# Covariance made the other way round and scaled by a row from DRAM, in place of a turn on TensorE

## The chip, the cores and the metric

The kernel runs on one core of a Trainium2 chip. Its time is the device time of one execution in microseconds (us); lower is better. The engines are PE (TensorE), DVE (VectorE), ACT (ScalarE), POOL (GpSimd) and SP (SyncE, which here only issues DMAs). Each takes its own instructions in program order; semaphores order them between engines.

## The reference

Two layers, one after the other, for 4 batches of 6208 rows with 256 channels, in float32:

```python
qn = q / (norm(q, axis=1) + 1e-06)             # norms down the 6208 rows, one for each channel
kn = k / (norm(k, axis=1) + 1e-06)
s  = kn.transpose(0, 2, 1) @ qn / tau           # [4, 256, 256], tau = 1
a  = softmax(s, axis=-1)
x  = v @ a                                      # [4, 6208, 256]

x_prev = x shifted down by one row
xk = mu_k * x + (1 - mu_k) * x_prev
xr = mu_r * x + (1 - mu_r) * x_prev
out = sigmoid(xr @ w_r) * (relu(xk @ w_k) ** 2 @ w_v)      # w_k 256 x 1024, w_v 1024 x 256, w_r 256 x 256
```

The softmax of a batch needs all rows of its q and k, and no row of x of that batch can be made before it.

## The kernel before

Batch 0 is handled by itself at the start. After that the kernel goes through 48 blocks of 512 rows (12 in a batch) and one short block of the rows left over. The order of all work is written out by hand: for each block `i` there are 8 slots `j`, and in each slot the main loop calls a fixed list of small pieces. A slot takes about 1.2 us, a block about 9.6 us.

For a block, `x_half` multiplies the turned v by the softmax (`xT_ps`, L458, with `a_sb` as the weights), ACT moves the result to SBUF (L460), DVE makes `delta` (L539), `xk` and `xr` (L549), `up` makes one eighth of the first product (`kT_ps`, L564), ACT applies relu (`kr`, L569), DVE squares (`kk`, L577), `down` makes the second product and the gate (`vr_ps`, L592 and L596), and `finish` combines them (ACT L605, DVE L606). Stores (L613) and the DMA transpositions of v (L410) go through SP's queue; loads of v (L402) and of q and k (L133) through POOL's. `x_half` of block n is called in slots 0 and 2 of step n-2, so it runs ahead of the rest of its block. `xT_ps`, `bank` and `st_ps` share two buffers of PSUM; `vr_ps` has two, `kT_ps` three.

The covariances of batches 1 to 3 are spread between the blocks of the batch ahead: `unit_matmul` adds 128 rows at a time into `s_ps` (L293), with q as the weights, so that S has q's channels down the partitions and k's along the columns. `unit_square` (ACT) and the adds on DVE gather the sums of squares.

When the last unit of a batch is through, `softmax_pieces` gives a list of small pieces (`chain`), and each following slot runs one of them, ahead of the slot's other work:

```python
        return [evac, None, norms, roots, pow2, None, invert, None, None, turn, lambda: exp([0]), lambda: exp([1]),
                shares, lambda: weigh(0), lambda: weigh(1)]
```

`evac` copies S from PSUM to `s_sb` (ACT, L346). `norms` sums the squares over the partitions on PE (L309), `roots` copies them to `rn` (ACT, L313), `pow2` takes the root on POOL (L335). `invert` adds 1e-6, takes the reciprocal (DVE, L338 and L339), and scales the rows of `s_sb` by q's inverse norms (L341, twice). `turn` transposes `s_sb` in four matmuls against the identity into `st_ps` (L353), so that k's channels lie down the partitions. `exp` reads `st_ps` with k's inverse norms as the scale of each partition (ACT, L361), and its sums go to `sm`. `shares` inverts the sums (DVE, L366), and `weigh` writes one half of `a_sb` (ACT, L370). `None` is a slot in which the chain does nothing. The chain also pauses when it has `NORMS` pieces left until the sums of squares are complete.

Of the kernel before, what the change touches and what calls it, by code (L numbers as in the profile page):

```python
# [10 lines left out]
F32 = mybir.dt.float32  # L11
BF16 = mybir.dt.bfloat16
AX = mybir.AxisListType.X
AF = mybir.ActivationFunctionType
OP = mybir.AluOpType
# [3 lines left out]
def kernel(  # L19
# [13 lines left out]
    nc = tc.nc  # L33
    B, N, C = q.shape
    D = C
    DF = moe_w_k.shape[1]
    P = 128
# [12 lines left out]
    pn = ctx.enter_context(tc.tile_pool(name="pn", bufs=2))  # L50
    p2 = ctx.enter_context(tc.tile_pool(name="p2", bufs=3))
    ps = ctx.enter_context(tc.tile_pool(name="ps", bufs=1, space=bass.MemoryType.PSUM))
    ctx.enter_context(tc.manual_schedule())

    ident = const.tile([P, P], BF16, name="ident")
# [23 lines left out]
    st_ps = {}  # L79
# [10 lines left out]
    def sizes(b):  # L90
        return [1] + [S] * (NB - 1) + [S // 2] * 2 if b == 0 else [1] + [S] * NB

    def order(b):
        g = list(range(len(sizes(b))))
        return [1, 2, 0] + g[3:]

    def rows_of(b, g):
        return (P if g else L), sizes(b)[g]
# [8 lines left out]
    def apart(b, g):  # L107
        return b == 1 and g > 0

    def rows_at(qk, b, g, i):  # L110
        if apart(b, g):
            return qk.rearrange("p s i c -> p (s i c)").rearrange("p (i s c) -> p i s c", i=2, s=S)[:, i]
        return qk[:, :, i]
# [169 lines left out]
    def unit_matmul(b, g, s):  # L283
        rows, n = rows_of(b, g)
        t0 = g == order(b)[0] and s == 0
        te = g == len(sizes(b)) - 1 and s == n - 1
        if t0:

            cov[b] = ps.tile([P, 2, C], F32, name="s_ps", tag="s_ps")
        s_ps = cov[b]  # L290
        qk = groups[b, g][0]
        for ih in range(2):
            nc.tensor.matmul(s_ps[:, ih, :], rows_at(qk, b, g, 0)[:rows, s, ih * P:(ih + 1) * P],  # L293
                             rows_at(qk, b, g, 1)[:rows, s, :], start=t0 and ih == 0, stop=te,
                             skip_group_check=True)
    def softmax_pieces(b):

        s_ps = cov.pop(b) if b else None
        rn = pn.tile([P, 4], F32, name="rn")
        s_sb = pn.tile([P, 2, C], F32, name="s_sb")  # L300
        e_sb = pn.tile([P, 2, C], F32, name="e_sb", bufs=1)
        mx = pn.tile([P, 2], F32, name="mx")
        sm = pn.tile([P, 2], F32, name="sm")
        rk = rn[:, 2:4]
        def norms():
            bank[b] = ps.tile([P, 4], F32, name="bank", tag="xT_ps", bufs=2)
            t = sums.pop(b)
            for i in range(4):
                nc.tensor.matmul(bank[b][:, i:i + 1], t[:, i * P:(i + 1) * P], ones[:, 0:1],  # L309
                                 start=i == 0, stop=True, skip_group_check=True)  # L310

        def roots():
            nc.scalar.copy(rn, bank[b])  # L313

        def diagonals():
            dg = pn.tile([P, 2, P], F32, name="dg", tag="dg", bufs=1)
            for h in range(2):
                nc.vector.scalar_tensor_tensor(dg[:, h], cov[0][h][:, 3 * P * h:3 * P * h + P], 1.0, ident_f,
                                               op0=OP.mult, op1=OP.mult, accum_out=rn[:, h:h + 1])

        def root(h):
            nc.scalar.activation(rn[:, 2 * h:2 * h + 2], bank[0][:, 0:2] if h else rn[:, 0:2], AF.Sqrt)

        def invert_first(h):
            nc.vector.tensor_scalar_add(rn[:, 2 * h:2 * h + 2], rn[:, 2 * h:2 * h + 2], 1e-6)
            nc.vector.reciprocal(rn[:, 2 * h:2 * h + 2], rn[:, 2 * h:2 * h + 2])
            if h and inv_tau != 1.0:
                nc.vector.tensor_scalar_mul(rk, rk, inv_tau)

        def evac_first():  # L330
            for h in range(2):
                nc.vector.tensor_scalar_mul(s_sb[:, h], cov[0][h][:, P:P + C], rn[:, h:h + 1])

        def pow2():
            nc.gpsimd.tensor_tensor(rn, rn, half, op=OP.pow)  # L335

        def invert():
            nc.vector.tensor_scalar_add(rn, rn, 1e-6)  # L338
            nc.vector.reciprocal(rn, rn)  # L339
            for h in range(2):  # L340
                nc.vector.tensor_scalar_mul(s_sb[:, h], s_sb[:, h], rn[:, h:h + 1])  # L341
            if inv_tau != 1.0:
                nc.vector.tensor_scalar_mul(rk, rk, inv_tau)

        def evac():
            nc.scalar.copy(s_sb, s_ps)  # L346

        def turn():

            st_ps[b] = ps.tile([P, 2, C], F32, name="st_ps", tag="xT_ps", bufs=2)  # L350
            for n in range(4):
                ih, dh = divmod(n, 2) if b else (n % 2, n // 2)
                nc.tensor.transpose(st_ps[b][:, ih, dh * P:(dh + 1) * P], s_sb[:, dh, ih * P:(ih + 1) * P],  # L353
                                    ident_f)

        def exp(halves=range(2)):
            for ih in halves:
                if not bounded:
                    nc.vector.tensor_reduce(mx[:, ih:ih + 1], st_ps[b][:, ih], axis=AX, op=OP.max, negate=True)
                    nc.vector.tensor_tensor(mx[:, ih:ih + 1], mx[:, ih:ih + 1], rk[:, ih:ih + 1], op=OP.mult)  # L360
                nc.scalar.activation(e_sb[:, ih], st_ps[b][:, ih], AF.Exp, scale=rk[:, ih:ih + 1],  # L361
                                     bias=0.0 if bounded else mx[:, ih:ih + 1],
                                     accum_out=sm[:, ih:ih + 1])

        def shares():
            nc.vector.reciprocal(sm, sm)  # L366

        def weigh(ih):
            ready.add((b, ih))
            nc.scalar.activation(a_sb[:, b, ih, :], e_sb[:, ih], AF.Copy, scale=sm[:, ih:ih + 1])  # L370

        def weigh_first(ih):
            nc.vector.reciprocal(sm[:, ih:ih + 1], sm[:, ih:ih + 1])
            nc.vector.tensor_scalar_mul(a_sb[:, b, ih, :], e_sb[:, ih], sm[:, ih:ih + 1])

        if b == 0:
            return diagonals, root, invert_first, evac_first, turn, exp, weigh_first

        return [evac, None, norms, roots, pow2, None, invert, None, None, turn, lambda: exp([0]), lambda: exp([1]),
                shares, lambda: weigh(0), lambda: weigh(1)]  # L380

    blocks = [(b, t) for b in range(B) for t in range(NB)] + ["left"]
    NBLK = len(blocks)
# [269 lines left out]
    def keep_warm(n):  # L653

        junk_ps = ps.tile([P, M], F32, name="junk_ps", tag="kT_ps", bufs=3)
        for _ in range(n):
            nc.tensor.matmul(junk_ps, ones, fill, start=True, stop=True)

    diagonals, root, invert_first, evac_first, turn, exp, weigh_first = softmax_pieces(0)
    pending = []  # L660
    for g in (1, 3, 5):
# [36 lines left out]
            pos["ld"] += 1  # L698

    chain = []  # L700
    NORMS = 13
    holds = [0]
    added = [0]

    def unit(ahead=2):

        if pos["mm"] >= len(units):
            return
        u = units[pos["mm"]]
        loads_upto()  # L710
        feed(max(ahead, 1))
        unit_matmul(*u)
        pos["mm"] += 1
        feed(ahead)
        if u[1:] == (NB, S - 1):
            chain.extend(softmax_pieces(u[0]))
            holds[0] = u[0]
# [46 lines left out]
    for i in range(-2, NBLK - 1):  # L764
        for j in range(8):
# [7 lines left out]
            if chain:  # L773
                piece = chain[0]
                if len(chain) == NORMS and (any(e[1] == holds[0] for e in adds) or now[0] < added[0] + 3):
                    piece = None
# [23 lines left out]
            if 0 < i + 2 < NBLK:  # L800
                n = i + 2
# [19 lines left out]
            if i == -1 and j in (5, 6):  # L821
                for u in early[:2] if j == 5 else early[2:]:
                    unit_matmul(*u)
# [60 lines left out]
```

## Time and profile before

| what | value |
|---|---|
| runs | 504.22 us median of 3 (503.79 to 505.19) |
| the profiled execution | 503.88 us, its span 502.1 us |
| TensorE clock granted | full over the whole span |
| PE / DVE / ACT / POOL busy | 96% / 85% / 85% / 19% of the span |
| DMA, mean over the span | 166 GB/s in 131542 packets |

The span is what the hardware profiler saw of one execution; about 1.8 us lie around it. A busy share is an average over the whole span: between about 45 and 495 us PE is busy almost without a gap, at the start it waits for the inputs. In the timelines two starts in a row on an engine can lie closer together than the first one's length, since instructions overlap in part; what an instruction takes away from its engine is the time to the next start.

### The profile page before, as it was taken

The page shows a single profiled execution, that of the slowest core. Times are in us where ns is not written, and L with a number is a line of the kernel's source. Part 1 is how long each engine was busy: PE and PEld are TensorE (multiplying, and loading weights), DVE is VectorE, ACT ScalarE, POOL GpSimd, SP SyncE. Part 2 cuts the span into 40 slices and gives each one's busy share as a digit, 9 for nine tenths or more (in the row PEclk, how much of TensorE's full clock was granted, in tenths as well). Part 3 has the DMA queues.
Part 4 walks back from the last instruction along what each step waited for, and adds up shares of the span by engine and source line. Part 5 has one row for each costly group of instructions (what it writes and reads, how often), then busy time and mean ns, then how long its engine had stood idle before and what let it go on. Part 6 is the DMA issues. An engine that isn't in the chain of part 4 may idle for free.

```text
span 502.1 us, 9301 instructions
## 1 busy us (share of the span) xinstructions
PE 481.3 (96%) x3437; PEld 331.0 (66%) x3437; DVE 428.4 (85%) x786; ACT 428.7 (85%) x872; POOL 96.6 (19%) x142
## 2 busy tenths in 40 slices
PE   1789999999999999999999999999999999999996
PEld 0355677667666766766776676676666666666675
DVE  2778899999988998998989899899898787878794
ACT  3789998999899889889998898998888888788884
POOL 0043421222333132121223323100031010000000
PEclk9999999999999999999999999999999999999999
DMA  8999999999799999997599999972296657345123
GB/s 325 418 315 197 201 193 174 211 208 199 146 184 184 200 168 180 148 196 121 139 188 154 190 175 180 177 140 64 75 198 104 152 90 153 77 107 85 58 69 106
DMA packets 131542, 83.46 MB, mean 166 GB/s; under 512 B 50532, under 2 KB 125608, under 8 KB 130472
## 3 DMA queue, kind: packets, MB, share of 16 engines
q0 software_dynamic: 55824, 33.01, 49.7%
q1 hardware_dynamic: 75352, 49.59, 40.0%
q8 instruction: 27, 0.44, 0.4%
q10 hardware_dynamic: 320, 0.26, 0.2%
q14 instruction: 19, 0.16, 0.1%
HBM read 78.71 MB, written 25.43 MB: 207 GB/s over the span
## 4 chain that ended last, share of the span: by engine, by line
PE 91%; DMA 4%; ACT 2%; DVE 1%; issue 1%; SPq 1%; ACTq 0%; DVEq 0%
PE vr_ps L596 33%; PE kT_ps L564 33%; PE vr_ps L592 8%; PE xT_ps L458 8%; PE s_ps L293 6%; DMA f<-in_k_dram 3%; ACT k L160 1%; DMA v_bf<-in_v_dram 1%; SPq L125 1%; ACT qk L155 0%; PE y_ps L636 0%; PE st_ps L353 0%; DVE k L167 0%; PE kT_ps L504 0%; DVE k L170 0%
## 5 line engine op out<-in xcount | busy, mean ns | idle before, releaser
L569 ACT ACTIVATE kr<-kT_ps 128x512 bf16<-128x512 f32 (+1 forms) x390 | 234.5, 604 | 33.2 <-PE kT_ps L564 29.5
L596 PE MATMUL vr_ps<-w_v_sb,kk 128*128 128x256 bf16 x1536 | 230.3, 273 | 0.0
L564 PE MATMUL kT_ps<-xk,w_k_sb 128*128 128x512 bf16 (+1 forms) x780 | 229.8, 377 | 0.0
L596 PEld LDWEIGHTS <-kk 128*128 128x128 bf16 x1536 | 150.3, 98 | 57.3
L577 DVE TENSOR_TENSOR kk<-kr 128x2048 bf16<-128x2048 bf16 (+1 forms) x148 | 125.6, 850 | 0.2 <-ACT kr L569 0.2
L606 DVE SCALAR_TENSOR_TENSOR res<-res,vr_ps 128x256 f32<-128x256 f32 x192 | 79.8, 416 | 50.1 <-ACT res L605 50.1
L564 PEld LDWEIGHTS <-w_k_sb 128*128 128x128 bf16 x780 | 75.5, 98 | 27.5 <-issue 0.6
L605 ACT ACTIVATE res<-vr_ps 128x256 f32<-128x256 f32 x192 | 76.5, 398 | 1.3 <-PE vr_ps L596 1.3
L592 PE MATMUL vr_ps<-w_r_sb,xr 128*128 128x256 bf16 x384 | 73.3, 273 | 0.0
L460 ACT CAST xT<-xT_ps 128x512 bf16<-128x512 f32 x94 | 55.9, 595 | 20.0 <-PE xT_ps L458 19.6
L549 DVE SCALAR_TENSOR_TENSOR xk<-delta,mu_t,xT 128x512 bf16<-128x512 bf16 x94 | 69.9, 745 | 0.0
L549 DVE SCALAR_TENSOR_TENSOR xr<-delta,mu_t,xT 128x512 bf16<-128x512 bf16 x94 | 69.9, 745 | 0.0
L592 PEld LDWEIGHTS <-xr 128*128 128x128 bf16 x384 | 37.6, 98 | 44.6 <-issue 0.2
L133 POOL DMA_DIRECT2D qk<-in_q_dram x39 | 26.1, 669 | 168.2 <-ACT kr L569 138.2
L458 PE MATMUL xT_ps<-vT,a_sb 128*128 128x512 bf16 x188 | 55.9, 379 | 0.0
L293 PE MATMUL s_ps<-qk 128*128 128x256 bf16 (+1 forms) x294 | 55.8, 273 | 0.0
L402 POOL DMA_DIRECT2D v_bf<-in_v_dram x48 | 36.6, 764 | 97.0 <-DMA vT<-v_bf 47.9
L254 ACT ACTIVATE sq<-qk 128x1024 bf16<-128x1024 bf16 x48 | 51.0, 1063 | 0.0
L199 PE MATMUL s_ps<-qk 128*128 128x384 bf16 (+2 forms) x98 | 20.0, 355 | 15.1 <-ACT qk L155 15.1
L539 DVE TENSOR_TENSOR delta<-xT 128x1024 bf16<-128x1024 bf16 x47 | 32.2, 685 | 0.7 <-ACT xT L460 0.7
L293 PEld LDWEIGHTS <-qk 128*128 128x128 bf16 (+1 forms) x294 | 28.5, 98 | 5.6 <-issue 0.8
L133 POOL DMA_DIRECT2D qk<-in_k_dram x39 | 25.9, 665 | 3.8 <-DMA w_k_sb<-in_moe_w_k_dram 2.4
(113 smaller groups left out, 249.5 us busy)
## 6 DMA issues: line engine op xcount, KB each, us to landing
out_dram<-res SPq DMA_DIRECT2D x47, 512.0 KB, 4.8
v_bf<-in_v_dram POOLq DMA_DIRECT2D x48, 256.0 KB, 7.1
qk<-in_q_dram POOLq DMA_DIRECT2D x36, 256.0 KB, 6.2
qk<-in_k_dram POOLq DMA_DIRECT2D x36, 256.0 KB, 7.8
f<-in_q_dram SPq DMA_DIRECT2D x4, 1024.0 KB, 13.4
f<-in_k_dram SPq DMA_DIRECT2D x4, 1024.0 KB, 11.0
f<-in_q_dram SPq DMA_DIRECT2D x3, 512.0 KB, 7.7
f<-in_k_dram SPq DMA_DIRECT2D x3, 512.0 KB, 6.1
```

The lines of the kernel that those rows point to most:

```text
L133: nc.gpsimd.dma_start(rows_at(qk, b, g, i)[:rows, :n], qk_src(t, b, g))
L293: nc.tensor.matmul(s_ps[:, ih, :], rows_at(qk, b, g, 0)[:rows, s, ih * P:(ih + 1) * P], rows_at(qk, b, g, 1)[:rows, s, :], start=t0 and ih ...
L458: nc.tensor.matmul(xT_ps, a_sb[:, b, ih, dh * P:(dh + 1) * P], vT[:, :, ih, :], start=ih == 0, stop=ih == 1)
L460: nc.scalar.copy(xT[:, dh, 1:], xT_ps)
L549: nc.vector.scalar_tensor_tensor(o[:, dh], st[i, "d"][:, dh], mu[:, dh:dh + 1], st[i, "x"][:, dh, :M], op0=OP.mult, op1=OP.add)
L564: nc.tensor.matmul(kT_ps[:, :m], w_k_sb[:, dh, fh * P:(fh + 1) * P], xk[:, dh, :m], start=dh == 0, stop=dh == 1)
L569: nc.scalar.activation(kr, kT_ps[:, :m], AF.Relu, scale=0.5 ** 0.5)
L577: nc.vector.tensor_tensor(st[i, "kk"][:, fh // 4 * 4 + lo:fh + 1, :m], kr, kr, op=OP.mult)
L592: nc.tensor.matmul(vr_ps[:, D:], xr[:, dh, s * P:(s + 1) * P], w_r_sb[:, dh, :], start=dh == 0, stop=dh == 1)
L596: nc.tensor.matmul(vr_ps[:, :D], kk[:, fh, s * P:(s + 1) * P], w_v_sb[:, fh, :], start=fh == 0, stop=fh == 7)
L605: nc.scalar.activation(res[:, s], vr_ps[:, D:], AF.Tanh, scale=0.5)
L606: nc.vector.scalar_tensor_tensor(res[:, s], res[:, s], 1.0, vr_ps[:, :D], op0=OP.add, op1=OP.mult)
```

## The change

For batches 1 to 3 the operands of the covariance matmuls are exchanged, so that S comes out with k's channels down the partitions and q's along the columns. It needs no turn, and `exp` reads it from `s_sb`. q's inverse norms now belong to the columns: `invert` writes them from `rn` to a row of 256 numbers in DRAM, and reads that row back to all 128 partitions (`rq`), with two DMAs on SP's queue. Five slots after `invert`, a new piece `spread` multiplies `s_sb` by `rq` on DVE, in one instruction. The two scalings in `invert` go. The two `exp` follow `spread`, `shares` and the first `weigh` are joined in one piece, and the chain has 16 pieces instead of 15. Batch 0 is unchanged.

```diff
+    scratch = ctx.enter_context(tc.tile_pool(name="scratch", bufs=2, space=bass.MemoryType.DRAM))
...
         for ih in range(2):
-            nc.tensor.matmul(s_ps[:, ih, :], rows_at(qk, b, g, 0)[:rows, s, ih * P:(ih + 1) * P],
-                             rows_at(qk, b, g, 1)[:rows, s, :], start=t0 and ih == 0, stop=te,
+            nc.tensor.matmul(s_ps[:, ih, :], rows_at(qk, b, g, 1)[:rows, s, ih * P:(ih + 1) * P],
+                             rows_at(qk, b, g, 0)[:rows, s, :], start=t0 and ih == 0, stop=te,
                              skip_group_check=True)
...
+        rq = pn.tile([P, C], F32, name="rq", tag="rq", bufs=1) if b else None
...
         def invert():
             nc.vector.tensor_scalar_add(rn, rn, 1e-6)
             nc.vector.reciprocal(rn, rn)
-            for h in range(2):
-                nc.vector.tensor_scalar_mul(s_sb[:, h], s_sb[:, h], rn[:, h:h + 1])
+            row = scratch.tile([1, 2 * P], F32, name="row", tag="row", bufs=2)
+            nc.sync.dma_start(row.rearrange("o (h p) -> p (o h)", p=P), rn[:, 0:2])
+            nc.sync.dma_start(rq, row.to_broadcast([P, 2 * P]))
...
+        def spread():
+            nc.vector.tensor_tensor(s_sb, s_sb, rq.unsqueeze(1).to_broadcast([P, 2, C]), op=OP.mult)
...
         def exp(halves=range(2)):
+            src = s_sb if b else st_ps[b]
             for ih in halves:
...
-                nc.scalar.activation(e_sb[:, ih], st_ps[b][:, ih], AF.Exp, scale=rk[:, ih:ih + 1],
+                nc.scalar.activation(e_sb[:, ih], src[:, ih], AF.Exp, scale=rk[:, ih:ih + 1],
...
-        return [evac, None, norms, roots, pow2, None, invert, None, None, turn, lambda: exp([0]), lambda: exp([1]),
-                shares, lambda: weigh(0), lambda: weigh(1)]
+        def shares_first():
+            shares()
+            weigh(0)
+
+        return [evac, None, norms, roots, pow2, None, invert, None, None, None, None, spread, lambda: exp([0]),
+                lambda: exp([1]), shares_first, lambda: weigh(1)]
...
-    NORMS = 13
+    NORMS = 14
```

More of the change, by code (lines that the diff above doesn't have):

```diff
@@ L351, in turn @@
             for n in range(4):
-                ih, dh = divmod(n, 2) if b else (n % 2, n // 2)
+                ih, dh = n % 2, n // 2
                 nc.tensor.transpose(st_ps[b][:, ih, dh * P:(dh + 1) * P], s_sb[:, dh, ih * P:(ih + 1) * P],
@@ L356, in exp @@
         def exp(halves=range(2)):
+            src = s_sb if b else st_ps[b]
             for ih in halves:
                 if not bounded:
-                    nc.vector.tensor_reduce(mx[:, ih:ih + 1], st_ps[b][:, ih], axis=AX, op=OP.max, negate=True)
+                    nc.vector.tensor_reduce(mx[:, ih:ih + 1], src[:, ih], axis=AX, op=OP.max, negate=True)
                     nc.vector.tensor_tensor(mx[:, ih:ih + 1], mx[:, ih:ih + 1], rk[:, ih:ih + 1], op=OP.mult)
-                nc.scalar.activation(e_sb[:, ih], st_ps[b][:, ih], AF.Exp, scale=rk[:, ih:ih + 1],
+                nc.scalar.activation(e_sb[:, ih], src[:, ih], AF.Exp, scale=rk[:, ih:ih + 1],
                                      bias=0.0 if bounded else mx[:, ih:ih + 1],
```

## The prediction

> **What bounds the kernel now.** I read the page first. Busy shares and the chain of waits say the same: TensorE.
>
> ```profile
> PE 481.3 (96%) x3437; PEld 331.0 (66%) x3437; DVE 428.4 (85%) x786; ACT 428.7 (85%) x872; POOL 96.6 (19%) x142
> PE 91%; DMA 4%; ACT 2%; DVE 1%; issue 1%; SPq 1%; ACTq 0%; DVEq 0%
> ```
>
> Between about 45 and 495 us PE never waits, so every microsecond taken from or added to its row there moves the end one for one. The forecast is thus a balance of removed PE work and new PE waits. The removed work, from the groups of the tile st_ps (min/median/max ns):
>
> ```profile
> L353 PE MATMUL st_ps<-ident_f,s_sb x16: 272/273/280, 37.5 to 369.5; 128*128 128x128 f32 x16
> ```
>
> Then I went to the stretch where batch 1's softmax ends, in the timelines of PE, DVE and ACT (start, length):
>
> ```profile
> 142.64 0.42 DVE L606 SCALAR_TENSOR_TENSOR res<-res,vr_ps 128x256 f32<-128x256 f32 x1 [1.49 <-ACT res L605]
> 145.72 0.16 DVE L366 RECIPROCAL sm<-sm 128x2 f32<-128x2 f32 x1
> 145.97 0.51 ACT L370 ACTIVATE a_sb<-e_sb,sm 128x256 bf16<-128x256 f32 x1 [0.24 <-DVE sm L366]
> 147.13 0.51 ACT L370 ACTIVATE a_sb<-e_sb,sm 128x256 bf16<-128x256 f32 x1
> 148.06 0.59 PE L458 MATMUL xT_ps<-vT,a_sb 128*128 128x512 bf16 x2
> ```
>
> The reader is to see how little is left: the second half of a_sb ends at 147.64, and the first matmul pair of batch 1's first block (L458, which loads a_sb as weights) starts at 148.06. That is 0.42 us of slack; and ACT has already waited 0.24 us for DVE's reciprocal. The same reading gives 1.79 us for batch 2 (262.04 against 263.83) and 1.83 us for batch 3 (376.04 against 377.87).
>
> Last, the DMA answer for single stores of 512 KB issued by SP at 140.5, 256.7, 371.3 and, on quiet engines, 362.6 us (last number: us to landing):
>
> ```profile
> out_dram<-res SPq DMA_DIRECT2D x1, 512.0 KB, 9.4
> out_dram<-res SPq DMA_DIRECT2D x1, 512.0 KB, 6.6
> out_dram<-res SPq DMA_DIRECT2D x1, 512.0 KB, 4.9
> out_dram<-res SPq DMA_DIRECT2D x1, 512.0 KB, 3.1
> ```
>
> The same transfer takes three times as long when POOL's loads fill the engines, as they do just where the new transfers go.
>
> [...] the trace agrees (64 KB stores at the end of the kernel land in 2.0 to 2.3 us). [...]
>
> **The change, part by part.**
>
> *Operands swapped (L293).* 294 matmuls of 128x256 stay 294 of the same shape, 273 ns: 0.
>
> *turn() gone for batches 1 to 3.* Four transposes started at 139.69 and the next matmul at 140.13: 0.44 us on PE. Three batches: **-1.3 us**, all on the path. exp reads s_sb in SBUF instead of st_ps: same ACT op, 0 taken (ACT isn't the bound). A PSUM buffer comes free; PE never waited for it, 0.
>
> *Scaling.* Two tensor_scalar (L341, 0.69 us start to next start) leave DVE; one f32 tensor_tensor 128x512 comes in five slots later: 0.61 us start to start, from L277. Amount about equal, but the place matters. Before, the scaling ran ahead of a DVE idle of 1.49, 1.29 and 1.18 us (the waits of L606 for ACT). The new one runs behind that idle, so it delays all that follows on DVE by its full length.
>
> *The chain is one slot longer and its middle moves.* spread, exp, exp sit two slots later than turn, exp, exp; shares and the first weigh share one; the second weigh is one slot (about 1.2 us) later. In the changed order the reciprocal of sm stands behind spread, the 2048-wide kk, two xk, res, and in batch 1 also a 1024-wide kk, a square sum and another res. DVE works in order, so I add start-to-start times from the timeline: res 0.34, delta 0.61, spread 0.61, kk 1.14, xk 0.66, res 0.33, xk 0.66, kk 0.60, sum 0.60, res 0.33.
>
> Batch 1, were the row there in time: DVE takes L606 at 142.25 (ACT is 0.4 earlier without turn), spread at 143.2, the reciprocal at 148.15 to 148.3 instead of 145.72. On ACT the first weigh waits for it till 148.35; then kr 0.48, sq 0.95, and the second weigh ends near 150.75. PE, 0.44 earlier, wants it for its second matmul of the pair at 147.84 (148.06 + 0.22 - 0.44). Wait: **2.95 us**.
> Batch 2: L606 258.15, spread 258.5, reciprocal ends 262.65; weigh 0.40, kr 0.47, res 0.27, weigh to 264.4, wanted 263.6: **0.8 us**.
> Batch 3: L606 372.65, spread 373.0, reciprocal ends 377.15; the second weigh ends 378.95, wanted 377.65: **1.3 us**.
> Together 5.05, and with the -1.3 this is +3.75. Behind the waiting PE stand all its later matmuls, which nobody can overtake; ACT and DVE only catch up in this time.
>
> *The row through DRAM.* Per batch two more DMAs on SP's queue: 256 pieces of 4 bytes out, then 128 rows of 1 KB back, the second issued only when the first has landed. Budget from the end of the reciprocal of rn to spread: 137.77 to 143.2, 252.55 to 258.5, 368.08 to 373.0, that is 5.4, 5.95 and 4.9 us. Cost from below: two quiet DMAs at 2.1 = 4.2 us, it fits and the lateness is 0 (early arrival gains nothing, DVE gets there no sooner). Cost with the traffic of the place: a 512 KB store is 32 rows of 1 KB for each engine; over the quiet 3.1 us each row pays (9.4 - 3.1)/32 = 0.20, 0.11 and 0.056 us. The new pair is 16 + 8 pieces for each engine: 4.2 + 24 x that = 8.9, 6.8, 5.55 us; with 0.1 for the issue it is late by 3.6, 0.95 and 0.75: 5.3 us. While DVE waits in spread, kk, xk and res stand behind it, and the reciprocal moves by the same amount, so it adds to PE's wait in full. From above: 0.20 per piece in all three batches (or short writes that cost more than rows) gives 3.6 + 3.05 + 4.1 = 10.7. I take three quarters of 5.3, **4.0 us**, because the store that was part of the crowd now stands behind the pair in SP's queue.
> SP: the row waits behind a transposition already issued (132.06, 247.36, 363.13) and holds back a store and the next transposition by some 2 to 6 us in batch 1, less later. That transposition (141.73, 9.3 us) is for a block whose L458 comes at 157.8: cover enough. POOL's order is unchanged.
>
> *Sum*: -1.3 + 5.05 + 4.0 = +7.75. The profiled execution took 503.88 (span 502.1 and 1.78 around it): 511.6. The median of the runs shown is 0.34 above it: **512.0 us**.
>
> **Rivals.** (a) The row arrives in time, only DVE's order bites: +3.75, 508.0. For it: two quiet DMAs fit. Against: the loads issued at 136.7 to 138.9 took 7 to 11.5 us. (b) Not slower: the slots cover everything and only the transposes count, -1.3, 502.9. It needs the second weigh by 147.84, 263.6 and 377.65, that is, DVE running 0.8 to 2.95 us less far behind PE than the trace shows; it decides if the reciprocal gets through before about 145.3, 261.85 and 375.85. If only batches 2 and 3 are covered, it is 505.9. (c) Crowded DMA in all batches: -1.3 + 5.05 + 10.7 = +14.4, 518.6. (d) That the change doesn't do what it says can be left out: the transposes are gone from PE's order.
>
> **How the numbers follow.** Late row 0.58, (a) 0.26, (b) with its partial forms 0.09, (c) 0.07. A measurement of this kernel tells about 0.3% (1.5 us) from no change; even (b) in full is only 0.26% faster, so faster gets 0.02, same 0.08, slower 0.90. The likeliest case spans 509 to 516; with (a) and most of (c) 506 to 518.
>
> **What would show it.** PE L458 waiting on ACT a_sb at the first block of each batch, most in batch 1; ACT's first weigh waiting on DVE sm; DVE's spread waiting on a DMA of rq, 3 us or so in batch 1; PE's matmul count down by 12. No wait at spread would leave (a). No wait before L458 would make the prediction wrong, as would a wait at another place (vT late, kk late).

## The result, and the profile after

The changed kernel took 541.17 us (median; 539.56 to 542.58) against 504.26 us: a ratio of 1.073, 95% interval 1.069 to 1.076. The prediction had 512.0, at most 518. The direction was right, and so was DVE's wait for the row; the size was four to five times what was forecast, and PE stops in other places than those that were named. Each kernel has its own line numbers: the matmuls into xT_ps are at L458 before and at L469 after. The profiled execution has a span of 540.7 us, 38.6 more than before.

The page of the kernel after: busy times, granted clock by slice, and the chain that ended last.

```profile
PE 488.3 (90%) x3425; PEld 332.4 (61%) x3425; DVE 429.5 (79%) x783; ACT 429.8 (79%) x872; POOL 96.5 (18%) x142
PEclk9999999999969999999987999999996999999999
PE 77%; DMA 13%; DVE 6%; ACT 2%; issue 1%; SPq 0%; ACTq 0%; DVEq 0%
```

The reader is to see three things. PE's idle time went from 20.8 to 52.4 us (span less busy time). DMA, 4% of the chain before, is 13% of it now. And the clock, full throughout before, dips three times; PE is busy 7.0 us longer than before with 12 matmuls fewer.

The kernel before has these waits of PE and no others, all at the start (waiter, releaser, us in total, times, longest):

```profile
PE s_ps L199 <- ACT qk L155: 15.1, 7, 10.1
PE vT_ps L438 <- DMA v_bf<-in_v_dram: 0.8, 1, 0.8
PE x_ps L481 <- DVE a_sb L374: 0.7, 1, 0.7
```

From the waits of the kernel after:

```profile
ACT e_sb L368 <- DVE s_sb L349: 32.0, 3, 11.6
DVE s_sb L349 <- DMA rq<-row: 30.5, 3, 11.4
...
PE kT_ps L575 <- ACT kr L580: 17.3, 2, 8.8
...
PE vr_ps L603 <- DVE res L617: 12.8, 3, 11.6
...
ACT a_sb L377 <- DVE sm L373: 3.4, 3, 1.6
...
PE xT_ps L469 <- ACT a_sb L377: 0.9, 1, 0.9
```

Read from the second line outwards: DVE stands in spread until rq lands, three times some 10 us. ACT stands in exp behind it, with kr in its queue. PE runs out of kT_ps or vr_ps buffers and stops, some 30 us in all. Batch 1 in the timelines of SP, DVE, ACT and PE:

```profile
138.21 0.37 SPq L343 DMA_DIRECT2D row<-rn  x1
150.51 0.34 SPq L344 DMA_DIRECT2D rq<-row  x1
...
155.18 0.69 DVE L349 TENSOR_TENSOR s_sb<-s_sb,rq 128x512 f32<-128x512 f32 x1 [11.45 <-DMA rq<-row]
...
160.12 0.16 DVE L373 RECIPROCAL sm<-sm 128x2 f32<-128x2 f32 x1
...
160.37 0.51 ACT L377 ACTIVATE a_sb<-e_sb,sm 128x256 bf16<-128x256 f32 x1 [1.62 <-DVE sm L373]
...
145.88 0.59 PE L575 MATMUL kT_ps<-xk,w_k_sb 128*128 128x512 bf16 x2
...
158.06 0.59 PE L603 MATMUL vr_ps<-w_r_sb,xr 128*128 128x256 bf16 x2 [11.59 <-DVE res L617]
...
159.50 1.06 PE L575 MATMUL kT_ps<-xk,w_k_sb 128*128 128x512 bf16 x2
...
162.76 0.39 PE L469 MATMUL xT_ps<-vT,a_sb 128*128 128x512 bf16 x1 [0.92 <-ACT a_sb L377]
```

The write of 1 KB holds SP from 138.21 to 150.51: 12.3 us; in batches 2 and 3 it is 11.8 and 9.4. The read back takes 4.6 and 4.7 us in batches 1 and 3; in batch 2 spread starts 4.0 us after its issue. When PE goes on, a pair of kT_ps matmuls takes 1.06 us instead of 0.59: the clock granted from 155 to 160 us is 0.50.

Where does the row spend 12 us? The packets of batch 1, from two windows of the DMA view, 142 to 144 and 144 to 146 us (q0 is POOL's queue, q1 SP's; packets, MB, share of 16 engines):

```profile
q0 software_dynamic: 686, 0.34, 129.7%
q1 hardware_dynamic: 261, 0.00, 14.6%
```
```profile
DMA packets 182, 0.09 MB, mean 45 GB/s; under 512 B 5, under 2 KB 182, under 8 KB 182
## 3 DMA queue, kind: packets, MB, share of 16 engines
q0 software_dynamic: 182, 0.09, 290.3%
```

The row's packets (these 261, and 11 in the two microseconds before) are on record by 144 us, among POOL's, which still run at full pace (686, and 671 in the two microseconds before). The landing comes at 150.5. In between POOL's packets crawl: 182 in two microseconds instead of 686, though by the records they fill the engines' time. From 143.5 to 150.2 us the engines move 50 GB/s, in the kernel before 202 (SP's own transfers among them, which here stand behind the row). So the row does not wait in line behind the loads; it rather looks as if the loads wait behind the row, which experiments 7 and 8 test.

### The profile page after: what moved, and what is told of

Its sections match the earlier page's. It is cut to its first block, busy times and chain, and to the rows that moved or that the text cites. A ratio compares the mean times of both kernels' runs of the same rounds, so it can differ in the third digit from the quotient of the medians.

```text
span 540.7 us, 9280 instructions
## 1 busy us (share of the span) xinstructions
PE 488.3 (90%) x3425; PEld 332.4 (61%) x3425; DVE 429.5 (79%) x783; ACT 429.8 (79%) x872; POOL 96.5 (18%) x142
## 4 chain that ended last, share of the span: by engine, by line
PE 77%; DMA 13%; DVE 6%; ACT 2%; issue 1%; SPq 0%; ACTq 0%; DVEq 0%
PE vr_ps L607 28%; PE kT_ps L575 28%; PE vr_ps L603 7%; PE xT_ps L469 7%; DMA row<-rn 6%; PE s_ps L294 5%; DMA f<-in_k_dram 3%; DMA rq<-row 2%; DVE kk L588 1%; DVE xk L560 1%; DMA v_bf<-in_v_dram 1%; ACT k L161 1%; DVE res L617 1%; DVE delta L550 1%; ACT qk L156 1%
## 5 line engine op out<-in xcount | busy, mean ns | idle before, releaser
L575 PE MATMUL kT_ps<-xk,w_k_sb 128*128 128x512 bf16 (+1 forms) x780 | 232.9, 381 | 17.3 <-ACT kr L580 17.3
L607 PE MATMUL vr_ps<-w_v_sb,kk 128*128 128x256 bf16 x1536 | 233.1, 275 | 0.0
L603 PE MATMUL vr_ps<-w_r_sb,xr 128*128 128x256 bf16 x384 | 74.2, 275 | 12.8 <-DVE res L617 12.8
L469 PE MATMUL xT_ps<-vT,a_sb 128*128 128x512 bf16 x188 | 57.1, 385 | 0.9 <-ACT a_sb L377 0.9
L368 ACT ACTIVATE e_sb<-s_sb,rn 128x256 f32<-128x256 f32 x6 | 3.0, 505 | 32.0 <-DVE s_sb L349 32.0
## 6 DMA issues: line engine op xcount, KB each, us to landing
out_dram<-res SPq DMA_DIRECT2D x47, 512.0 KB, 4.9
f<-in_q_dram SPq DMA_DIRECT2D x3, 512.0 KB, 7.6
f<-in_k_dram SPq DMA_DIRECT2D x3, 512.0 KB, 6.2
```

What stands on the lines that cost most here:

```text
L469: nc.tensor.matmul(xT_ps, a_sb[:, b, ih, dh * P:(dh + 1) * P], vT[:, :, ih, :], start=ih == 0, stop=ih == 1)
L575: nc.tensor.matmul(kT_ps[:, :m], w_k_sb[:, dh, fh * P:(fh + 1) * P], xk[:, dh, :m], start=dh == 0, stop=dh == 1)
L603: nc.tensor.matmul(vr_ps[:, D:], xr[:, dh, s * P:(s + 1) * P], w_r_sb[:, dh, :], start=dh == 0, stop=dh == 1)
L607: nc.tensor.matmul(vr_ps[:, :D], kk[:, fh, s * P:(s + 1) * P], w_v_sb[:, fh, :], start=fh == 0, stop=fh == 7)
```

## The experiments

Ten runs. The theory after the result was: the lateness of the row, 30.5 us, plus what a standing PE loses, is the whole excess; and the row is late because short writes into the same few lines of DRAM wait for each other. Rivals: another part of the change costs; the pieces wait behind POOL's loads; each short write has a price wherever it goes.

**1. No row at all.**

```diff
+    nc.vector.memset(rq_const, 0.0125)
...
-        rq = pn.tile([P, C], F32, name="rq", tag="rq", bufs=1) if b else None
+        rq = rq_const if b else None
...
-            row = scratch.tile([1, 2 * P], F32, name="row", tag="row", bufs=2)
-            nc.sync.dma_start(row.rearrange("o (h p) -> p (o h)", p=P), rn[:, 0:2])
-            nc.sync.dma_start(rq, row.to_broadcast([P, 2 * P]))
```

> The changed kernel without its two DMAs: spread multiplies by a constant tile instead of rq, so the output is scaled wrongly, but each engine has the same instructions. Theory (the row's lateness, 30.5 us at spread, and what PE loses by standing still): what is left is DVE's order, 2.95 + 0.8 + 1.3 us of PE wait less 1.3 us of transposes, +3.75 us, so 508 us; full clock throughout. Rival (the operand swap, the f32 product or the order of the chain is the larger cost): 520 us or more.

508.33 us, ratio 1.009 (1.006 to 1.011). That is +4.5 us, against +3.75 worked out. The waits of this kernel:

```profile
ACT a_sb L375 <- DVE sm L371: 3.4, 3, 1.6
PE xT_ps L467 <- ACT a_sb L375: 3.3, 4, 1.4
```

But for the start and 0.4 us at vr_ps, PE waits only where the prediction said, at the first block of a batch for ACT's weigh, which waits for DVE's reciprocal. From the starts of the xT_ps pairs against before, batch 1 loses 3.0 us (2.95 worked out), batch 2 0.7 (0.8) and batch 3 1.25 (1.3). Of the four executions two took 507.2 and 507.3 us, at a mean clock of 0.999 and 1.000, and two 509.4 and 509.6, at 0.995 and 0.996; the profiled one is the first, 3.4 us over before. Full clock throughout, which was expected, is thus shown for two of four. By the medians about 33 of the 37 us belong to the two DMAs and what they set off.

**2. The chain of before, still without the row.**

```diff
-        return [evac, None, norms, roots, pow2, None, invert, None, None, None, None, spread, lambda: exp([0]),
-                lambda: exp([1]), shares_first, lambda: weigh(1)]
+        return [evac, None, norms, roots, pow2, None, invert, None, None, spread, lambda: exp([0]),
+                lambda: exp([1]), shares, lambda: weigh(0), lambda: weigh(1)]
...
-    NORMS = 14
+    NORMS = 13
```

> The run without the row (spread by a constant, so the output is scaled wrongly), with the chain of before: spread in turn's slot, ahead of DVE's idle, exp, shares and weigh in their old slots. Theory (the 4.5 us over before that the run without the row showed are DVE's order): PE's waits at xT_ps vanish, 1.3 us under before, 502.3 to 503.3 us. Rival (they come from the operand swap or from exp reading SBUF): 507 us or more.

503.13 us, ratio 0.9981 (0.9973 to 0.9988): no wait at xT_ps. So what experiment 1 lost is the place of the pieces in the chain, and with it the order on DVE, not the swap or the source of exp (0.51 us from SBUF in the changed kernel, 0.48 from PSUM in the one before). The gain is 0.8 us, or 0.95 by the ratio, not 1.3: the starts of the xT_ps pairs show PE losing 0.16 us in batch 2 and 0.55 us in batch 3 again within ten microseconds of the saving.

**3. The pieces 512 bytes apart.**

```diff
-            nc.sync.dma_start(row.rearrange("o (h p) -> p (o h)", p=P), rn[:, 0:2])
-            nc.sync.dma_start(rq, row.to_broadcast([P, 2 * P]))
+            nc.sync.dma_start(spaced.rearrange("(h p) w -> p h w", p=P)[:, :, 0:1], rn[:, 0:2].unsqueeze(2))
+            nc.sync.dma_start(rq, spaced.rearrange("c w -> (c w)")[0:2 * P].unsqueeze(0).to_broadcast([P, 2 * P]))
```

> The changed kernel with the 256 numbers of the row written 512 bytes apart in DRAM[...], and the first 1 KB of that read back, so the values are not the norms; a fill of the 128 KB at the start is added. Same number of pieces, same order. Theory A (short writes into the same few lines of DRAM wait for each other): row lands in 4 to 6 us, the wait at spread falls to 1 to 4 us a batch, total 510 to 522 us. Theory B (the pieces wait behind POOL's loads) and theory C (each short write has its price wherever it goes): row still 9 to 12 us, total 538 to 545 us.

522.58 us, ratio 1.037 (1.035 to 1.040), just above the range of theory A and far below that of the others.

```profile
DVE s_sb L350 <- DMA rq<-spaced: 11.4, 3, 4.4
```

The wait at spread falls from 30.5 to 11.4 us with the same number of pieces among the same loads. Theories B and C, in which only number and crowd count, had expected no change. The write now lands in 6.0 us at the longest and the read in 2.9 to 3.8, so a row through DRAM is late here even when it doesn't lie packed.

**4. Series of writes by themselves.** Two kernels append single writes to the kernel before, each finished before the next: after each write comes a read into `m`, for which the next write waits. One of the forms:

```diff
     last_block(NBLK - 1)
...
+    def packed(name):
+        d = draw(name, [1, 2 * P])
+        nc.sync.dma_start(d.rearrange("o (h p) -> p (o h)", p=P), m[:, 0:2])
+        nc.sync.dma_start(m, d.to_broadcast([P, 2 * P]))
```

> The kernel before, followed by a series of writes to DRAM from SP, each read back before the next starts: 256 pieces of 4 bytes packed in 1 KB (twice), 128 of 8 bytes packed, 256 of 4 bytes 512 bytes apart, the same 64 bytes apart, 16 of 64 bytes, 2 of 512 bytes; once on quiet DMA engines, once beside a stream of loads from POOL. Theory A (same lines): quiet, packed 6 us or more, 512 apart 2 to 3 us, 64 and 512 bytes 2 us. Theory B (crowd): all quiet ones near 2 us, all crowded ones 5 us or more. Theory C (price of a piece): quiet, both packed and apart 6 us or more, the pairs half of the excess.

> The kernel before, followed on quiet engines by single writes of 4-byte pieces from SP, each finished before the next: 256 pieces packed, 8, 16, 32 and 64 bytes apart; then packed with 128 pieces (one column of 128 partitions), with 64 partitions of two, with 16 partitions of two; packed again. Theory (pieces in the same line wait for each other, by number): packed 8.4 us, falling with the spacing to 1.6 us at 64 bytes; 128 pieces 4 to 5 us, 32 pieces near 2 us. Rival (only pieces of different DMA engines collide): 16 partitions of two still well over 2 us in proportion to what they share, and the fall with spacing sudden.

The time from a write's issue to the next instruction on SP's queue, which waits for it to land. Four starts of the first kernel's SP timeline show how it is read (8.4 us packed, 1.6 us 512 bytes apart):

```profile
512.68 0.36 SPq L860 DMA_DIRECT2D pk0b<-m  x1
521.12 0.34 SPq L861 DMA_DIRECT2D m<-pk0b  x1
...
533.64 0.37 SPq L871 DMA_DIRECT2D spw<-m  x1
535.21 0.33 SPq L872 DMA_DIRECT2D m<-spw  x1
```

| write | quiet, us | beside POOL's loads, us |
|---|---|---|
| 256 pieces of 4 bytes, packed | 8.4, 8.4, 8.5, 8.1 | 9.0, 8.6 |
| 8 bytes apart | 3.3 | |
| 16, 32, 64, 512 bytes apart | 1.6, 1.7, 1.6, 1.6 | 5.1 (64), 4.9 (512) |
| 128 pieces of 8 bytes, packed | 3.1 | 6.8 |
| 128 of 4 bytes, packed (128 partitions) | 8.0 | |
| 128 of 4 bytes (64 partitions of two) | 7.3 | |
| 32 of 4 bytes (16 partitions of two) | 1.3 | |
| 16 of 64 bytes / 2 of 512 bytes | 1.3 / 1.1 | 4.3 / 4.0 |

Packed neighbours cost 6.8 us over the same pieces 16 bytes or more apart, on quiet engines. The crowd adds 3.3 to 3.5 us to a spaced write and little to the packed one. But the crowd is not the same: POOL's loads begin only with the first packed write, and in the page's slice of 16 us around the second the engines move 110 GB/s, in those around the spaced ones 181 and 192. The 128 pieces from 64 partitions and the 32 lie in two packed runs each, 512 bytes apart. The expectation that the price falls with the number was wrong: half the pieces, packed, cost nearly as much, and 32 cost nothing.

**5. Whose pieces collide?**

```diff
+        columns(f"across{k}", m[0:16, 0:16], lambda d: d.rearrange("o (h p) -> p (o h)", p=16))
+        columns(f"within{k}", m[0:16, 0:32:2], lambda d: d.rearrange("o (p h) -> (o p) h", h=16))
+        columns(f"whole{k}", m[0:16, 0:16], lambda d: d.rearrange("o (p h) -> (o p) h", h=16))
```

> The kernel before, followed on quiet engines by single writes of 1 KB from SP, twice each: 256 pieces of 4 bytes from 16 partitions with neighbours in DRAM from different partitions (across), the same with neighbours from the same partition (within; the source takes every second column, so that nothing merges), and 16 pieces of 64 bytes (whole). Theory (a DMA engine's own pieces collide when they are neighbours[...]): across 1.3 to 2 us, within 8 us or more, whole 1.3 us. Rival (pieces of different engines collide in a line): across 8 us or more, within 2 us.

`columns` takes a name, the source and the view of the row that is written. Across 6.9 and 6.3 us, within 7.1 and 7.1, whole 1.3 and 1.3. Neither theory: neighbours of 4 bytes are slow whether they come from one partition or from different ones. Which DMA engine takes which partition, on which both theories rest, is not shown by these runs.

**6. The row in the kernel before, read back but unused.**

```diff
             nc.vector.reciprocal(rn, rn)
+            row = scratch.tile([1, 2 * P], F32, name="row", tag="row", bufs=2)
+            nc.sync.dma_start(row.rearrange("o (h p) -> p (o h)", p=P), rn[:, 0:2])
+            nc.sync.dma_start(rq, row.to_broadcast([P, 2 * P]))
             for h in range(2):
                 nc.vector.tensor_scalar_mul(s_sb[:, h], s_sb[:, h], rn[:, h:h + 1])
```

> The kernel before, with the two DMAs of the row added where the change has them, but nobody reads rq. Theory (only the wait for the row costs): 504 to 505 us; row still lands after 9 to 12 us. Rival (the short writes clog the DMA engines, so POOL's loads of q, k and v come late and PE waits for them): 506 us or more, with new waits of ACT or PE on DMAs.

521.69 us, ratio 1.036 (1.033 to 1.040): the theory that only the wait at spread costs is refuted. The rival's number holds, and PE does wait for a DMA, though not for POOL's loads. What it waits for is v, turned by SP's DMA:

```profile
PE xT_ps L463 <- DMA vT<-v_bf: 12.7, 2, 8.0
```

SP waits 12.4 us for the row in batch 1, so the transposition behind it starts at 152.04 instead of 141.73, and PE meets its lateness at 157.8 us. The transposition in this kernel and in the kernel before:

```profile
152.04 5.28 SPq L415 DMA_TRANSPOSE vT<-v_bf  x1
```
```profile
141.73 3.93 SPq L410 DMA_TRANSPOSE vT<-v_bf  x1
```

**7. The write alone, unread.**

```diff
+            row = scratch.tile([1, 2 * P], F32, name="row", tag="row", bufs=2)
+            nc.sync.dma_start(row.rearrange("o (h p) -> p (o h)", p=P), rn[:, 0:2])
```

> The kernel before with the row's write alone, in the place where the change has it; nothing reads it, so SP waits for nothing more than before and its queue isn't held. Theory (clog: while the packed writes drain, POOL's loads and the transpositions of v crawl on the same engines): vT lands late and PE waits for it as with the unread row, 512 to 522 us. Rival (SP's queue, held by the read back's wait for the row, was what made vT late): 504 to 506 us.

509.28 us, ratio 1.009 (1.007 to 1.011), below the range of the theory and above that of the rival. SP doesn't wait for the row, the transposition starts on it at 141.53 as before, and yet (the kernel before in the second fence):

```profile
vT<-v_bf SPq DMA_TRANSPOSE x1, 20.6
```
```profile
vT<-v_bf SPq DMA_TRANSPOSE x1, 9.3
```
```profile
PE xT_ps L461 <- DMA vT<-v_bf: 4.4, 1, 4.4
```

It lands after 20.6 us instead of 9.3, and SP spends 11.97 us on it instead of 3.93; from 143.5 to 150.2 us the engines move 31 GB/s, before 202. So the packed write clogs the engines by itself (+5.3 us, once in three batches), and the rest of the 18 us of experiment 6 comes with the read back. That it is the held queue that costs there, and not the 128 KB that are read, is seen in the starts above, but was not tried by itself.

**8. The write alone, 16 bytes apart.**

```diff
-            row = scratch.tile([1, 2 * P], F32, name="row", tag="row", bufs=2)
-            nc.sync.dma_start(row.rearrange("o (h p) -> p (o h)", p=P), rn[:, 0:2])
+            row = scratch.tile([2 * P, 4], F32, name="row", tag="row", bufs=2)
+            nc.sync.dma_start(row.rearrange("(h p) w -> p h w", p=P)[:, :, 0:1], rn[:, 0:2].unsqueeze(2))
```

> The kernel before with the unread write of the row, its 256 pieces 16 bytes apart instead of packed. Theory (it is the collision of packed pieces that clogs the engines, not their number): row lands in 3 to 6 us, vT isn't late, 503.5 to 505 us. Rival (any 256 short writes among POOL's loads do it): 508 to 510 us as with the packed write.

503.68 us, ratio 0.9998 (0.9989 to 1.0007). The row lands in 6.5 to 7.0 us, a little over the 3 to 6 expected, and costs nothing. POOL's packets from 144 to 146 us, in this kernel and in that of experiment 7:

```profile
q0 software_dynamic: 506, 0.25, 96.4%
```
```profile
q0 software_dynamic: 89, 0.04, 183.3%
```

The transposition lands after 9.3 us as before, and from 144 to 146 us the engines move 209 GB/s, in the kernel before 219. With the neighbours apart the clog is gone.

**9. The norms spread on TensorE.**

```diff
+            for h in range(2):
+                nc.vector.tensor_scalar_mul(dgq[:, h], ident, rn[:, h:h + 1])
...
+            nc.tensor.matmul(rq, ones, dgq.rearrange("p h c -> p (h c)"), start=True, stop=True)
```

> The changed kernel with no DRAM: invert makes the diagonal of q's inverse norms (identity times rn, bf16, two DVE instructions), one matmul of ones against it (128x256, 0.11 us) puts them along the columns in all partitions, and spread multiplies by that, in the slot where turn was; exp, shares and weigh in their slots of before. Theory (the row through DRAM and DVE's order are the whole loss): 0.44 - 0.11 = 0.33 us a batch less than before, 503.0 to 504.0 us, no wait of PE at xT_ps. Rival (something else in the change, the swap or the longer f32 product on DVE, costs): 505 us or more.

504.17 us, ratio 1.0003 (0.9993 to 1.0013): as fast as before, not faster. The rival of 505 or more is out, but the forecast gain didn't come. PE is 0.33 us earlier after each batch's matmul, and gives 0.48 us (batch 2) and 0.81 us (batch 3) back soon after:

```profile
PE vr_ps L600 <- DVE res L614: 1.0, 2, 0.7
```

PE stands there for want of a vr_ps buffer, which DVE hasn't read out yet. So it seems that ACT and DVE are as far behind as PE's buffers allow, and an earlier PE only waits; the two waits, 0.3 and 0.7 us, are less than the 0.48 and 0.81.

## Why the prediction was wrong

- **The price of the row failed.** The term was 8.9, 6.8 and 5.55 us for write and read together. Measured: 16.9, about 15.7 and 14.1. DVE waited 11.45, 9.83 and 9.21 us at spread, where 3.6, 0.95 and 0.75 had been worked out. Taken apart by its 16 and 8 pieces, it has the write at 5.25, 3.85 and 3.0 us, which took 12.3, 11.8 and 9.4, and the read at 3.65, 3.0 and 2.55, which took 4.6, about 4.0 and 4.7. The error was to price a 4-byte piece by its count, with a 1 KB row as the nearest thing. Quiet, such a packed write takes 8.4 us (experiment 4), and no store of the kernel before could show it. The prediction did name short writes that cost more than rows, in its bound from above, but gave them no price of their own. The upper bound, 10.7 us of lateness, came from the same rows, so the range had no place for 30.5. A bound "from above" has to come from another mechanism than the value that it bounds.
- **The quiet base held.** The 2.1 us for a quiet DMA were not the error: at the end of the kernel before, SP's 64 KB stores land in 2.3 us and ACT's in 2.0, and on quiet engines the small writes of experiment 4 that lie whole, or 16 bytes or more apart, land in 1.1 to 1.7.
- **The discount of a quarter**, for a store that now stands behind the pair, could not help: the packed write takes 8.1 to 8.5 us with no crowd at all, and 8.6 to 9.0 beside POOL's loads.
- **The place of PE's wait failed.** The prediction had it at xT_ps, at the first block of each batch, and named a wait at another place as a sign against itself. PE stops at kT_ps (17.3 us) and vr_ps (12.8); at xT_ps it waits once, 0.9 us. The prediction saw that kk, xk and res stand behind DVE's wait, but not that PE then has no free buffer of kT_ps or vr_ps before it gets to xT_ps. The other signs came: DVE's wait for rq, ACT's first weigh waiting for sm, 12 matmuls fewer.
- **That lateness adds to PE's wait in full held in batch 1 alone.** There 11.45 us of wait at spread, with the 2.95 of DVE's order less 0.44, give 13.96. By the xT_ps pairs the kernel stands 0.42 us behind the one before ahead of this chain, and 14.50 behind it: 14.08. Batches 2 and 3 add 12.08 and 11.92 us, where 10.19 and 10.07 come out in the same way.
- **DVE's order held**: +3.75 worked out, 4.5 measured without the row by the medians and 3.4 in the profiled execution (experiment 1), and gone when the order is restored (experiment 2). In the changed kernel itself it shows as only 0.9 us at xT_ps, because PE stood earlier, at vr_ps and kT_ps.
- **A cost was missing: the clock.** 30.5 + 5.05 - 1.3 = 34.25 of the 38.6 us of span. Of the rest 0.4 us lie ahead of batch 1's chain, and 3.7 are what batches 2 and 3 add beyond the working. They come from PE's half clock after its stop. In batch 1 it is hidden, since PE has to wait for a_sb after all. In batch 2 the second weigh ends at 288.65, and PE gets to xT_ps 0.98 us later (ACT, PE, and the windows view, in which the clock is the third number from the end):

```profile
288.14 0.51 ACT L377 ACTIVATE a_sb<-e_sb,sm 128x256 bf16<-128x256 f32 x1
```
```profile
289.63 1.06 PE L469 MATMUL xT_ps<-vT,a_sb 128*128 128x512 bf16 x2
290.49 0.95 PE L575 MATMUL kT_ps<-xk,w_k_sb 128*128 128x512 bf16 x2
291.27 0.38 PE L603 MATMUL vr_ps<-w_r_sb,xr 128*128 128x256 bf16 x2
```
```profile
285.00:290.00 5.00, 4.40 (x17) 2.37 (x16) 4.82 (x11) 4.38 (x11) 1.54 (x3) 0.50 0.04 5
```

The two pairs from 289.63 take 1.64 us to the next start where at full clock they take 0.87. With the 0.98 that is 1.75 of batch 2's 1.89. After 4.52 us of waiting in experiment 3 the granted clock is 0.50, after 0.97 and 1.44 us in the profiled execution of experiment 1 it stays at 1.00; where it gives way, between 1.44 us of waiting and the 4.42 of experiment 7 (pairs at 1.06 us behind it), these runs do not show. The return took about 5 us here: PE works without a gap from 286.27, and is back at full clock at 291.27. From the windows view, 150 to 155 us, of experiment 3 and of experiment 1:

```profile
150.00:155.00 5.00, 3.88 (x15) 2.02 (x14) 4.89 (x11) 3.38 (x9) 1.70 (x3) 0.50 0.05 4
```
```profile
150.00:155.00 5.00, 4.47 (x30) 2.70 (x31) 1.94 (x4) 4.14 (x10) 2.24 (x3) 1.00 1.34 232
```

- **SP's cover was overrated.** "Cover enough" for the transposition behind the row was wrong in the kernel before (experiment 6): the transposition started 10.3 us later and then took 13.8 us instead of 9.3. In the changed kernel PE is so late by then that no wait for vT shows.
- **One for one failed in the small**: of 1.3 us of transposes removed, 0.8 to 0.95 arrived (experiment 2).

## What to carry to other kernels

What a write to DRAM cost in these runs depended on how its pieces lay there, not on bytes or pieces alone: on quiet engines 1 KB in packed 4-byte pieces took 8.1 to 8.5 us where spacing of 16 bytes or more, or 64-byte pieces, took 1.3 to 1.7, and while it drained beside POOL's loads it slowed them (89 packets from 144 to 146 us in experiment 7, 506 with the pieces 16 bytes apart) and the transposition of v (20.6 us instead of 9.3). Where a dependent pair of DMAs stands on one queue, look at what waits behind it on that queue, and at which in-order engine consumes the result. And spreading a vector along the columns needs no DRAM: one matmul of ones against a diagonal did it in 0.11 us of PE's time, with two instructions on DVE for the diagonal (0.33 us to the next start), though in a kernel with all three engines near their limits (PE, DVE and ACT busy 96%, 85% and 85%) it gained nothing.

## What the runs showed of the hardware that was not expected

- Neighbouring 4-byte writes to DRAM, packed: 8.1 to 8.5 us for 256, 8.0 for 128, 7.3 for 128 from 64 partitions, 1.3 for 32 (the last two in two packed runs). At 8 bytes apart 3.3, at 16 or more 1.6 to 1.7. The shortness of the pieces alone isn't the price, since single 4-byte pieces 512 bytes apart land in 1.6 us. Why neighbours collide, and why the price hardly depends on the number above some point, stays open.
- In the profile such a write's packets are on record microseconds before it lands: in batch 1 by about 144 us, with the landing at 150.5. Beside it, POOL's packets fell from 686 to 182 in two microseconds, and with the write alone, which doesn't hold back SP's transfers, all engines together from 202 to 31 GB/s (143.5 to 150.2 us).
- Half clock after a stop in the middle of a kernel of 4.4 us (experiment 7: pairs of kT_ps matmuls at 1.06 us instead of 0.59), 4.5 us (experiment 3: granted clock 0.50 from 150 to 155 us) and more. In the changed kernel the granted clock falls to 0.50 between 4.8 and 5.1 us after the end of PE's last matmul, and is back at 1.00 after 3.4, 4.9 and 5.1 us of work (from 158.06, 286.27 and 412.34). At the start of the kernel before, PE stands 10.1 us and the clock is on record as 1.00 all the same.
